# A planner with other latencies, loads that queue and an exclusion rule, and due times set by hand for 215 operations

## The chip, the cores and the metric

The kernel runs on one core of a Trainium2 chip. The metric is the device time of one execution in microseconds. Engines are named as the profile names them: PE is TensorE (PEld its weight loads), DVE is VectorE, ACT is ScalarE, POOL is GpSimd, SP is SyncE, which here issues nearly all DMAs (its queue is SPq in the rows).

## The reference, cut to what matters

A gated linear attention over 768 steps (4 batches, 8 heads, head size 48) feeds a two-layer network on 3072 tokens (384 to 2048 to 384), all in float32.

```python
for t in range(S):                       # S = 768
    cur = einsum('bhd,bhe->bhde', u * k_t, v_t)
    y[:, :, t] = einsum('bhd,bhde->bhe', r_t, state + cur)
    state = w_t[..., None] * state + einsum('bhd,bhe->bhde', k_t, v_t)
x = y.transpose(0, 2, 1, 3).reshape(3072, 384)
h = x @ w_in
g = maximum(h, 0) + alpha * minimum(h, 0)
out = g @ w_out
```

## The kernel before, in words

**Attention.** The 768 steps are cut in 12 blocks of 64, and two of the four batches are taken together, which gives 24 chunks q of 128 tokens. `load` (lines 385 to 398) fetches each chunk's decays (`wd`), keys and receptances in two layouts (`kr`, `rk`) and values (`nv`). `prep` runs two scans on DVE (lines 410 and 416), three or so products (406, 419, 422) and, from chunk 5 on, two products on POOL (440); ACT writes the diagonal blocks (`at`, 448). `scores`, `transposes` and `outputs` are bursts of small matmuls on PE (lines 467 and 513). For the first three chunks `spreads` (576) rearranges a part of the result on PE from a copy that ACT makes into `os` (579); the result goes to `x_0` (the tile `xw`, 589). POOL scales the running state (458).

**Network.** The hidden width is cut in 16 tiles j of 128. The weights come as 64-bit words, 768 KB a tile, into one of two buffers `raw` (line 634). ACT scales the low words in place (645), DVE makes the full weights `wf` from them in three passes (647, 650, 654). Later ACT copies the high part `wh` (665) and DVE makes the rest `wl` (666). Tokens are worked in 8 groups g of three chunks. Group 0 multiplies in plain float32 with `wf` (the units are listed in `FIRST`); groups 1 to 7 use three products of rounded parts, `wh`, `wl` and the two parts of x. A unit (g, j) is a product into the hidden tile (`moe_up`, PE line 684, three chunks wide), `pos` by ACT and DVE (689, 691), in groups 1 to 7 also `gh` and `gl` (695, 696), and two units later the product into the output (`moe_down`, line 709). `moe_out` copies and stores the result. `check_load` fetches decays and weights a second time, late in the program, for checks on ACT.

**What sets the order.** No engine's order is written out by hand. Each piece of work is declared by `op(engine, duration, function, reads, writes, ...)` of class `Plan` (line 107), which numbers it in the order of declaration, finds what it depends on from the keys it reads and writes, and gives it a due time where one is passed. The calls pass durations: 1.17 for a scan, 0.4 for an issue on SP, and `lat`, 2.2 for a weight tile. `order` (line 138) first hands due times back from each operation to those that it needs, then plays the program: at each moment each free engine starts, of the operations whose inputs are done, the one due first whose buffers are free. A load ends at `max(dma, end + DMA_LAT) + lat`, where `dma` is the end of the load before. Operations marked `lock` (DVE and POOL work that reads two tiles of SBUF) exclude one another on DVE and POOL. `order_late` (line 222) does this twice: after the first time each load is held back until `LEAD`, 10 us, before the planned start of the first operation that needs it. The resulting order of each engine is then emitted as it is: an engine runs its instructions strictly in that order, and waits at each for its inputs.

While the plan has PE idle before the first output product of chunk 2, filler matmuls on a constant tile are emitted (line 834, `FILL` and `FILL_MIN`), as many as the planned gap holds; at the start PE also runs 12 such matmuls (line 738).

Of the kernel before, what the change touches and what calls it, by code (L numbers as in the profile page):

```python
# [58 lines left out]
MODES = {("M", "Q"): 0.1, ("Q", "M"): 0.1}  # L59
DMA_LAT = 2.0  # L60
# [34 lines left out]
class Op:  # L95
    __slots__ = ("eng", "dur", "lat", "fn", "deps", "succ", "due", "lock", "takes", "uses", "kind", "n", "left",
                 "ready", "start", "after", "keys")


class Plan:  # L100
# [6 lines left out]
    def op(self, eng, dur, fn, r=(), w=(), lat=0.1, due=None, lock=False, kind=None, after=0.0):  # L107

        o = Op()
        o.eng, o.dur, o.lat, o.fn, o.due, o.lock, o.kind = eng, dur, lat, fn, due, lock, kind  # L110
        o.after = after
        o.n, o.deps, o.succ, o.takes, o.uses, o.start = len(self.ops), {}, [], [], [], None
        self.ops.append(o)
        o.keys = {*r, *w}
        keys = [(k if isinstance(k, tuple) else (k, None), k in w) for k in list(dict.fromkeys([*r, *w]))]
        for key, written in keys:
            t = key[0]
            if isinstance(t, Tensor) and t not in o.uses:
                o.uses.append(t)
                t.users += 1  # L120
                if t.first is None:
                    t.first = o.n
                    o.takes.append(t)
                else:
                    o.deps[t.first] = True
            if key in self.writer:
                o.deps[self.writer[key]] = True
            if written:
                for x in self.readers.get(key, ()):
                    o.deps.setdefault(x, False)  # L130
# [5 lines left out]
        o.deps.pop(o.n, None)  # L136
        return o

    def order(self):
        ops = self.ops  # L140
        for t in {t for o in ops for t in o.uses}:
            t.users = sum(t in o.uses for o in ops)
            t.ring.free, t.ring.given = list(range(len(t.ring.tiles))), 0
        for o in ops:
            o.succ = []
        for o in ops:
            for d in o.deps:
                ops[d].succ.append(o.n)
        for o in reversed(ops):
            late = [ops[s].due for s in o.succ if ops[s].deps[o.n]]  # L150
            late = min(late) - o.dur - o.lat if late else None
            o.due = late if o.due is None else o.due if late is None else min(late, o.due)
            if o.due is None:
                o.due = 1e6
        engines = ("PE", "DVE", "ACT", "POOL", "SP")
        free = dict.fromkeys(engines, 0.0)
        waiting = {e: [] for e in engines}
        ready = {e: [] for e in engines}
        ends, lock, dma, mode, now, todo = [], 0.0, 0.0, "M", 0.0, len(ops)
        for o in ops:  # L160
            o.left, o.ready = len(o.deps), o.after
            if not o.left:
                heapq.heappush(waiting[o.eng], (o.ready, o.n))
        while todo:
            while ends and ends[0][0] <= now:
                _, n = heapq.heappop(ends)
                for t in ops[n].uses:
                    t.users -= 1
                    if not t.users:
                        t.ring.free.append(t.slot)  # L170
            for e in engines:
                while waiting[e] and waiting[e][0][0] <= now:
                    _, n = heapq.heappop(waiting[e])
                    heapq.heappush(ready[e], (ops[n].due, n))
                if free[e] > now:
                    continue
                held, pick = [], None
                while ready[e]:
                    it = heapq.heappop(ready[e])
                    o = ops[it[1]]  # L180
                    if o.lock and (lock > now or e == "DVE" and any(
                            ops[n].lock and d < o.due for d, n in ready["POOL"] if free["POOL"] <= now)):
                        held.append(it)
                        continue
                    need = {}
                    for t in o.takes:
                        need.setdefault(t.ring, []).append(t)
                    if all(len(ts) <= len(g.free) and (not g.ordered or ts[0].ticket == g.given)
                           for g, ts in need.items()):
                        pick = o  # L190
                        break
                    held.append(it)
                for it in held:
                    heapq.heappush(ready[e], it)
                if pick is None:
                    continue
                o = pick
                for t in o.takes:
                    t.slot = t.ring.free.pop(0)
                    t.ring.given += 1  # L200
                o.start, dur, todo = now, o.dur, todo - 1
                if e == "PE":
                    dur += MODES.get((mode, o.kind[0]), 0.0)
                    mode = o.kind[1]
                end = now + dur
                free[e] = end
# [7 lines left out]
                heapq.heappush(ends, (end, o.n))  # L214
                for s in o.succ:
                    x = ops[s]
                    x.left -= 1
                    x.ready = max(x.ready, end)
                    if not x.left:
                        heapq.heappush(waiting[x.eng], (x.ready, s))  # L220
            if todo:
                assert any(t > now for t in free.values()) or ends or any(waiting.values()), "the rings are too short"
                times = [t for t in free.values() if t > now] + [w[0][0] for w in waiting.values() if w and w[0][0] > now]
                times += [ends[0][0]] if ends else []
                now = min(t for t in times if t > now)
        return sorted(ops, key=lambda o: (o.start, o.n))
# [11 lines left out]
def fast_path(tc, alpha_n, flag, dmaj, nat, u, ud, wts, alpha, out):  # L238
# [11 lines left out]
    with tc.tile_pool(name="const", bufs=1) as const, tc.tile_pool(name="psum", bufs=1, space=PSUM) as psum, \  # L250
# [13 lines left out]

        def w_low(j):
            if j not in wl:
                wl[j] = wpool.tile([P, 2, DM], F32R, name=f"wl{j}", tag=f"w{j - 1 if j else NF}")
# [29 lines left out]
        minus = const.tile([P, P], F32R, name="minus")  # L297
        r_pos = ring("pos", [P, GT], 3)
# [61 lines left out]

        def step(n):
# [3 lines left out]
            return (STEP if g > 0 else WHOLE) * (s1 - s0) / GS  # L365
# [34 lines left out]
        def prep(q):  # L400
# [27 lines left out]
            if q < U_BY_PE:  # L428
# [6 lines left out]
                op("PE", 0.9, sums, r=[rk, "u_dm"], w=[cp], kind="MM", due=due_att[q] - 3.5)  # L435
# [619 lines left out]
```

## Time and profile before

| what | value |
|---|---|
| runs | 508.67, 508.45, 504.23 us; median 508.45 us |
| profiled execution, first to last instruction | 507.8 us |
| median less this span | 0.65 us |
| instructions | 13048 |
| busy share of PE / DVE / ACT / POOL | 98% / 66% / 57% / 15% |
| moved by DMA | 72.40 MB, mean 143 GB/s |

The profile has no time of its own for the profiled execution beside the span. A busy share is an average over stages: PE can be busy at a lower granted clock or with fillers, and an engine that is 66% busy over the whole can have no free time in one stage. The views by stretch of time say which stage is which.

### The profile page before, as it was taken

Reading aid. Unit: us, or ns where it says so; the run is one execution under the profiler, and the core shown is the slowest. Engines: PE = TensorE matmul, PEld = TensorE weight load, DVE = VectorE, ACT = ScalarE, POOL = GpSimd, SP = SyncE. Lnnn points to the kernel's source line nnn. Section 1 sums busy time; section 2 is a strip of 40 time slices with the busy share of each in tenths; the row PEclk is TensorE's granted clock in tenths of the full one; section 3 lists DMA queues with packets and bytes.
Section 4 is the critical chain, followed back from the end, with each engine's and each line's share of the span. In section 5 each row is a group of like instructions: output and inputs, shape, how many; then the busy total and the mean of one; then the engine's idle time right before and its main releaser. Section 6 shows DMA issues by size and latency. Waiting matters only on the chain.

```text
span 507.8 us, 13048 instructions
## 1 busy us (share of the span) xinstructions
PE 496.1 (98%) x5406; PEld 458.7 (90%) x5406; DVE 337.6 (66%) x602; ACT 291.5 (57%) x746; POOL 74.0 (15%) x103
## 2 busy tenths in 40 slices
PE   8999998999999999999999999999999999999995
PEld 8876664689999999999999999999999999999995
DVE  6899997999987564956478474855556353443332
ACT  4866574563363535456585765776677676553331
POOL 2010333233014010222014020030000000000000
PEclk9999998999999999999999999999999999999999
DMA  8648884561163311736157461756445441210001
GB/s 300 234 179 294 298 297 166 181 185 43 43 178 86 104 52 65 185 99 224 60 171 215 126 207 46 258 168 205 146 140 196 139 159 63 71 44 21 1 3 52
DMA packets 27107, 72.40 MB, mean 143 GB/s; under 512 B 3680, under 2 KB 8224, under 8 KB 27040
## 3 DMA queue, kind: packets, MB, share of 16 engines
q1 hardware_dynamic: 26656, 71.19, 43.5%
q8 instruction: 44, 0.72, 0.6%
q10 hardware_dynamic: 384, 0.30, 0.2%
q14 instruction: 23, 0.19, 0.1%
HBM read 64.70 MB, written 4.72 MB: 137 GB/s over the span
## 4 chain that ended last, share of the span: by engine, by line
PE 70%; DVE 11%; DMA 9%; ACT 5%; issue 3%; SPq 2%; ACTq 0%; DVEq 0%
PE bank L684 31%; PE op L709 30%; DMA raw<-in_wts_dram 6%; PE bank L467 6%; DMA kr<-in_dmaj_dram 2%; ACT at L448 1%; DVE cx L650 1%; DVE wf L654 1%; DVE suf L410 1%; DVE pos L691 1%; DVE kr L419 1%; PE bank L513 1%; DVE gl L696 1%; DVE kr L422 1%; SPq L621 1%
## 5 line engine op out<-in xcount | busy, mean ns | idle before, releaser
L684 PE MATMUL bank<-x,wh 128*128 128x384 f32 x672 | 191.3, 338 | 0.0
L689 ACT ACTIVATE pos<-bank,alpha_n 128x384 f32<-128x384 f32 (+1 forms) x133 | 75.4, 569 | 104.5 <-PE bank L684 102.3
L691 DVE SCALAR_TENSOR_TENSOR pos<-bank,pos 128x384 f32<-128x384 f32 (+1 forms) x133 | 71.6, 538 | 89.4 <-ACT pos L689 89.2
L684 PEld LDWEIGHTS bank<-x,wh 128*128 128x128 f32 x672 | 123.0, 188 | 1.2
L709 PE MATMUL op<-wh,gl 128*128 128x384 f32 x336 | 113.0, 336 | 1.0 <-DVE gl L696 0.7
L709 PE MATMUL op<-wh,gh 128*128 128x384 f32 x336 | 113.1, 337 | 0.0
L709 PE MATMUL op<-wl,gh 128*128 128x384 f32 x336 | 112.5, 335 | 0.0
L684 PE MATMUL bank<-x,wl 128*128 128x384 f32 x336 | 112.4, 335 | 0.0
L696 DVE TENSOR_TENSOR gl<-pos,gh 128x384 fp32r<-128x384 f32 x112 | 67.1, 599 | 54.8 <-ACT gh L695 54.8
L695 ACT CAST gh<-pos 128x384 fp32r<-128x384 f32 x112 | 57.5, 514 | 53.5 <-DVE pos L691 52.7
L709 PEld LDWEIGHTS op<-wh,gl 128*128 128x128 f32 x336 | 63.1, 188 | 2.9 <-DVE gl L696 2.9
L709 PEld LDWEIGHTS op<-wh,gh 128*128 128x128 f32 x336 | 63.1, 188 | 0.1
L684 PEld LDWEIGHTS bank<-x,wl 128*128 128x128 f32 x336 | 63.1, 188 | 0.0
L709 PEld LDWEIGHTS op<-wl,gh 128*128 128x128 f32 x336 | 63.1, 188 | 0.0
L458 POOL TENSOR_TENSOR St<-St,pc_all 128x192 f32<-128x192 f32 x44 | 23.8, 562 | 248.7 <-DVE St L611 209.8
L448 ACT ACTIVATE at<-twin,cd 128x64 f32<-128x64 f32 x192 | 52.6, 343 | 0.9 <-PE bank L467 0.7
L684 PE MATMUL bank<-xw,wf 128*128 128x384 f32 (+2 forms) x126 | 35.9, 425 | 2.3 <-DVE wf L654 2.3
L709 PE MATMUL op<-wf,pos 128*128 128x384 f32 x96 | 35.4, 499 | 0.0
L410 DVE TENSOR_TENSOR_SCAN suf<-wd,low 128x528 f32<-128x528 f32 x24 | 30.9, 1287 | 3.9 <-DMA wd<-in_dmaj_dram 3.9
L416 DVE TENSOR_TENSOR_SCAN wd<-wd,low 128x528 f32<-128x528 f32 x24 | 33.4, 1391 | 0.1
L684 PEld LDWEIGHTS bank<-xw,wf 128*128 128x128 f32 x126 | 20.9, 193 | 13.1 <-DVE wf L654 3.1
L440 POOL TENSOR_TENSOR rk<-rk,u_bc 128x384 f32<-128x384 f32 x19 | 20.3, 1069 | 84.1 <-DMA rk<-in_nat_dram 49.3
(81 smaller groups left out, 530.0 us busy)
## 6 DMA issues: line engine op xcount, KB each, us to landing
raw<-in_wts_dram SPq DMA_DIRECT2D x32, 768.0 KB, 5.1
kr<-in_dmaj_dram SPq DMA_DIRECT2D x24, 512.0 KB, 3.9
rk<-in_nat_dram SPq DMA_DIRECT2D x19, 384.0 KB, 3.7
wd<-in_dmaj_dram SPq DMA_DIRECT2D x24, 264.0 KB, 2.8
raw<-in_dmaj_dram SPq DMA_DIRECT2D x12, 528.0 KB, 4.2
nv<-in_nat_dram SPq DMA_DIRECT2D x24, 256.0 KB, 4.9
out_dram<-os SPq DMA_DIRECT2D x44, 96.0 KB, 2.2
x<-x SPq DMA_DIRECT2D x28, 72.0 KB, 4.6
```

Source lines behind the costliest of these rows:

```text
L410: op("DVE", 1.17, lambda: nc.vector.tensor_tensor_scan(out=suf.ap[:, ::-1], data0=w.ap[:, ::-1], data1=low[:, ::-1], initial=0.0, op0=ALU. ...
L416: op("DVE", 1.17, lambda: nc.vector.tensor_tensor_scan(out=w.ap, data0=w.ap, data1=low, initial=0.0, op0=ALU.mult, op1=ALU.max), r=["low"] ...
L440: op("POOL", 1.0, lambda i=i: nc.gpsimd.tensor_tensor(out=rk.ap[:, 0:HD], in0=rk.ap[:, 0:HD], in1=u_bc if i == 0 else rk.ap[:, HD:], op=AL ...
L448: nc.scalar.activation(out=at.ap[:, o, p, :], in_=twin, func=AF.Copy, scale=cd.ap[:, o * NP + p:o * NP + p + 1])
L458: op("POOL", 0.6, lambda i=i: nc.gpsimd.tensor_tensor(out=St[b][:, i, :, 0:D], in0=St[b][:, i, :, 0:D], in1=pc_all[:, q, i::2].unsqueeze(2 ...
L467: nc.tensor.matmul(yb[q][i].ap[rows, cols], start=(i, rows.start) not in opened[q], stop=stop, skip_group_check=True, **kw)
L684: nc.tensor.matmul(hp.ap[:, ts], lhsT=a, rhs=b[:, k, ts], start=(i == 0), stop=(i == m - 1))
L689: op("ACT", 0.15 + 0.33 * share, lambda: nc.scalar.activation(out=pos.ap[:, ts], in_=hp.ap[:, ts], func=AF.Relu, scale=alpha_n[:, j:j + 1] ...
L691: op("DVE", 0.07 + 0.4 * share, lambda: nc.vector.scalar_tensor_tensor(out=pos.ap[:, ts], in0=hp.ap[:, ts], scalar=0.0, in1=pos.ap[:, ts], ...
L695: op("ACT", 0.43, lambda: nc.scalar.copy(out=gh.ap, in_=pos.ap), r=[pos], w=[gh])
L696: op("DVE", 0.47, lambda: nc.vector.tensor_tensor(out=gl.ap, in0=pos.ap, in1=gh.ap.bitcast(F32), op=ALU.subtract), r=[pos, gh], w=[gl], lo ...
L709: nc.tensor.matmul(ops_[s], lhsT=a.ap[:, ts], rhs=w, start=(j == 0 and i == 0), stop=(j == NF - 1 and i == len(todo) - 1))
```

## The change

A few of the planner's costs change (going from 64-wide to 128-wide matmuls, `spreads`, `transposes` and the first 12 matmuls); what follows an operation on another engine now waits for a lag by engine (`TAIL`), or for one given with the operation (`part`). A load's end is counted from its start, which for an issue of 0.4 us is the same as before. `order` is rewritten around a list of events, and POOL now comes before DVE: a POOL operation with `lock` is issued at once and starts when DVE's running one ends, and DVE starts no `lock` operation until 0.1 us before POOL's ends. `dues` adds a number of `TUNE` to the due time of 215 operations, counted in order of declaration, and hands it back to what they need. `LEADS` changes the 10 us of lead for six loads: 744 is the load of weight tile 0, 23 and 29 are values of chunks 1 and 3, 33 and 34 decays and keys of chunk 5, 35 is u. `THREE` is 16 (`NF`) and `APART` is empty, and with these values the new branches that use them compute what stood there before.

```diff
-MODES = {("M", "Q"): 0.1, ("Q", "M"): 0.1}
-DMA_LAT = 2.0
+MODES = {("M", "Q"): 0.1, ("Q", "M"): 0.08}
+DMA_LAT = 2.4
+TAIL = {"PE": 0.2, "DVE": 0.118, "ACT": 0.133, "POOL": 0.083, "SP": 0.033}
+TUNE = {
+    5: 5.64, 10: 5.26, 123: -7.58, 134: -6.64, 138: -11.21, 144: -0.6, 145: -9.26, 146: -1.09, 149: 16.13, 152: -13.79, 154:
...
+    2.32, 887: -12.08, 888: 2.78, 889: 2.15, 892: 15.07, 893: 1.44, 898: -5.37, 899: 2.18, 901: 10.36, 903: 4.39, 905: -1.46, 906:
...
+LEADS = {
+    23: -1.51, 29: -5.91, 33: 8.76, 34: -0.82, 35: 5.78, 744: -4.77,
+}
+APART = ()
+THREE = NF
...
+        def wait(n, data, key):
+            x = self.ops[n]
+            if n != o.n and not (x.eng == eng and eng != "SP"):
+                o.lag[n] = max(o.lag.get(n, -9.0), x.part.get(key[0], TAIL[x.eng]) if data else TAIL[x.eng])
...
+    def dues(self, tune):
...
+            late = min(late) - o.dur - o.lat if late else 1e6
+            o.due = min(late, 1e6 if o.own is None else o.own) + tune.get(o.n, 0.0)
...
-        engines = ("PE", "DVE", "ACT", "POOL", "SP")
+        engines = ("PE", "POOL", "DVE", "ACT", "SP")
...
-                if o.lock:
-                    lock = end
-                if e == "SP":
-                    dma = max(dma, end + DMA_LAT) + o.lat
-                    end = dma
-                else:
-                    end += o.lat + (0.15 if e == "PE" else 0.06)
...
+                    o.start, dur, todo = now, o.dur, todo - 1
+                    if o.lock and e == "POOL" and lock["DVE"] > now:
+                        o.start = lock["DVE"]
...
+                    if o.lock:
+                        lock[e] = end - (0.1 if e == "POOL" else 0.0)
+                        push(events, (lock[e], 2, "POOL" if e == "DVE" else "DVE"))
+                    if e == "SP":
+                        dma = max(dma, now + DMA_LAT) + o.lat
+                        end = dma
...
     def order_late(self, lead, until):
 
+        self.dues(TUNE)
         self.order()
...
-                o.after = max(o.after, need - lead)
+                o.after = max(o.after, need - lead - LEADS.get(o.n, 0.0))
...
-            op("PE", 0.45, products, r=[(kr, 0), "ident"], w=[kp, "kn"], kind="MM", due=due_att[q] - 3.0)
+            op("PE", 0.36, products, r=[(kr, 0), "ident"], w=[kp, "kn"], kind="MM", due=due_att[q] - 3.0, tag=("t", q))
...
-                op("PE", 0.75, spreads, r=[sp, (tmp, s % 2, 0), (tmp, s % 2, 1)], w=yb[q], kind="MM")
+                op("PE", 1.29, spreads, r=[sp, (tmp, s % 2, 0), (tmp, s % 2, 1)], w=yb[q], kind="MM", part={yb[q][0]: -0.45})
...
+        def place_low(j):
+            return NF if j == THREE % NF else (j - 1) % NF
...
+        def parted(g, j):
+            return g > 0 or j >= THREE
...
-        op("PE", 4.4, wm, r=[(tmp, "warm")], w=[wm_t], kind="MM", due=0.0)
+        op("PE", 4.5, wm, r=[(tmp, "warm")], w=[wm_t], kind="MM", due=0.0)
```

In this numbering 900 and 901 are the ACT and the DVE part of `pos` of unit (0, 11), 805, 807 and 808 the ACT pass (645), the second and the last DVE pass (650, 654) of weight tile 12, and 810 the ACT pass of tile 13.

## Rows read from the trace of the kernel before

**Rows 1.** The page, its first part: busy time, share, instructions.
```profile
span 507.8 us, 13048 instructions
...
PE 496.1 (98%) x5406; PEld 458.7 (90%) x5406; DVE 337.6 (66%) x602; ACT 291.5 (57%) x746; POOL 74.0 (15%) x103
```

**Rows 2.** Busy by stretch: from:to, length, engines' busy us (instructions), granted clock, DMA share, GB/s.
```profile
3.90:18.79 14.89, 13.50 (x270) 12.20 (x269) 14.81 (x24) 9.95 (x38) 0.44 (x6) 1.00 0.82 306
18.79:79.80 61.01, 60.78 (x672) 42.09 (x666) 56.53 (x94) 38.91 (x96) 14.20 (x16) 1.00 0.74 262
79.80:82.15 2.35, 0.04 (x1) 0.00 (x0) 1.48 (x3) 2.35 (x9) 0.00 (x0) 1.00 0.28 110
82.15:85.40 3.25, 3.25 (x7) 1.91 (x8) 3.25 (x4) 1.12 (x3) 2.57 (x2) 0.66 0.68 225
85.40:88.00 2.60, 2.60 (x8) 1.41 (x8) 2.60 (x4) 0.58 (x1) 0.00 (x0) 0.77 0.40 125
...
116.00:496.90 380.90, 379.85 (x4061) 371.60 (x4059) 229.38 (x426) 218.84 (x556) 44.91 (x55) 1.00 0.38 117
```

**Rows 3.** The chain that ended last, 70 to 86 us: start, length, what.
```profile
71.33 7.86 DMA raw<-in_wts_dram
...
79.27 0.91 ACT raw L645
80.18 0.47 ACT pos L689
...
81.15 0.96 DVE wf L654
```

**Rows 4.** Instructions of PE, 82 to 93 us: start, length, line, tiles, count.
```profile
82.15 3.23 PE L684 MATMUL bank<-xw,wf 128*128 128x384 f32 x6 [2.31 <-DVE wf L654]
...
87.82 0.55 PE L513 MATMUL bank<-ident,kr 112*128 112x112 f32 x4
88.20 2.11 PE L684 MATMUL bank<-xw,wf 128*128 128x384 f32 x6
90.15 2.10 PE L709 MATMUL op<-wf,pos 128*128 128x384 f32 x6
92.18 0.46 PE L467 MATMUL bank<-kr,St 64*64 64x64 f32 x16
```

**Rows 5.** Instructions of ACT and DVE in order of time, 72 to 78 us.
```profile
72.20 0.95 ACT L645 ACTIVATE raw<-raw 128x768 int32<-128x768 uint32 x1
...
73.91 1.69 DVE L650 SCALAR_TENSOR_TENSOR cx<-raw,cx 128x768 int32<-128x768 int32 x1
```

**Rows 6.** The chain that ended last, 3 to 18 us.
```profile
3.28 8.59 DMA raw<-in_wts_dram
...
11.90 0.95 ACT raw L645
...
15.74 0.19 ACT os L579 x2
```

**Rows 7.** Instructions of PE, 12 to 19 us.
```profile
12.54 0.69 PE L467 MATMUL bank<-at,nv 64*64 64x64 f32 x32
...
14.27 0.62 PE L834 MATMUL op<-os 128*128 128x128 f32 x4
15.96 1.52 PE L576 MATMUL bank<-os,os 128*128 128x64 f32 x12 [1.07 <-ACT os L579]
17.32 0.44 PE L834 MATMUL op<-os 128*128 128x128 f32 x2
...
18.79 0.94 PE L684 MATMUL bank<-xw,wf 128*128 128x128 f32 x6
```

**Rows 8.** DMA issues, 0 to 110 us: tiles, count, KB each, median us to landing.
```profile
raw<-in_wts_dram SPq DMA_DIRECT2D x16, 768.0 KB, 4.6
```

**Rows 9.** Instructions of DVE, 14 to 55 us: the last pass of tile 0, one blocked scan.
```profile
14.86 0.95 DVE L654 CUSTOM_DVE_ANT_0 wf<-raw,cx 128x1536 uint16<-128x1536 uint16 x1
...
54.22 2.04 DVE L410 TENSOR_TENSOR_SCAN suf<-wd,low 128x528 f32<-128x528 f32 x1
```

More of the change, by code (lines that the diff above doesn't have):

```diff
@@ L95 @@
 class Op:
[L96 to L97 removed]
+    __slots__ = ("eng", "dur", "lat", "fn", "deps", "lag", "succ", "due", "own", "lock", "takes", "uses", "kind", "n", "left",
+                 "ready", "start", "after", "keys", "tag", "part", "rings", "_a0")
 class Plan:
@@ L140, in order @@
+    def order(self, until=1e9):
         ops = self.ops
-        for t in {t for o in ops for t in o.uses}:
-            t.users = sum(t in o.uses for o in ops)
-            t.ring.free, t.ring.given = list(range(len(t.ring.tiles))), 0
+        rings = {}
         for o in ops:
-            o.succ = []
+            for t in o.takes:
+                t.users = 0
+                t.ring.free, t.ring.given = list(range(len(t.ring.tiles))), 0
         for o in ops:
-            for d in o.deps:
-                ops[d].succ.append(o.n)
@@ L156, in order @@
+            o.rings = list(need.items())
+            o.left, o.ready, o.start = len(o.deps), o.after, None
+        engines = ("PE", "POOL", "DVE", "ACT", "SP")
         free = dict.fromkeys(engines, 0.0)
-        waiting = {e: [] for e in engines}
         ready = {e: [] for e in engines}
-        ends, lock, dma, mode, now, todo = [], 0.0, 0.0, "M", 0.0, len(ops)
+        held = {e: [] for e in engines}
+        lock = {"DVE": 0.0, "POOL": 0.0}
+        dma, mode, todo, count = 0.0, "M", len(ops), 0
@@ L160, in order @@
+        events = []
         for o in ops:
-            o.left, o.ready = len(o.deps), o.after
             if not o.left:
-                heapq.heappush(waiting[o.eng], (o.ready, o.n))
+                events.append((o.ready, 0, o.n))
+        heapq.heapify(events)
+        push, pop = heapq.heappush, heapq.heappop
         while todo:
[L165 to L170, printed above, removed]
@@ L221, in order @@
[L221 to L226, printed above, removed]
+            now = events[0][0]
+            if now > until:
+                break
@@ new lines, in order @@
+            dirty = set()
+            while events and events[0][0] <= now + 1e-9:
+                _, what, n = pop(events)
+                if what == 0:
+                    e = ops[n].eng
+                    push(ready[e], (ops[n].due, n))
+                    dirty.add(e)
+                elif what == 1:
+                    for t in ops[n].uses:
+                        t.users -= 1
+                        if not t.users:
+                            t.ring.free.append(t.slot)
+                            dirty.update(engines)
+                else:
+                    dirty.add(n)
@@ L228, in order_late @@
+            if todo and not events:
+                assert False, "the rings are too short"
+        return sorted((o for o in ops if o.start is not None), key=lambda o: (o.start, o.n))
     def order_late(self, lead, until):
+        self.dues(TUNE)
         self.order()
@@ L702, in moe_down @@
             g, s0, s1, j = units[m]
+            three = parted(g, j)
             for s in range(s0, s1):
```

188 lines of the change are left out of this document (107 added, 81 removed), and 19 rows, old and new, of the table TUNE.

## The prediction

> **What bounds the kernel now.** I read the busy times of the whole span first, then the same by stretch, then the chain that ended last through the stretches where PE was not full, and at those places the engines in order of time. Over the whole, PE is busy for 496.1 of 507.8 us and, its own weight loads aside, no other engine for more than 337.6 [rows 1]. So the time is PE's work, plus what PE loses; a plan can win only the losses. By stretch there are three kinds of them [rows 2]. From 3.90 to 18.79 DVE is full (14.81 of 14.89) and prepares the first chunks and weight tiles; PE waits for it, with small work and fillers between. From 18.79 to 79.80 PE is full (60.78 of 61.01), and DVE nearly so (56.53). From 79.80 to 82.15 PE stands still, and then runs until 88.00 at a granted clock of 0.66 and 0.77. From 116.00 to 496.90 PE misses 380.90 - 379.85 = 1.05 us in all, too little to plan for.
>
> The stall at 79.80 is the place to understand. PE waits 2.31 us for the weights of tile 12 [rows 4]. Their inputs had long been there: ACT's pass over that tile began at 72.20, and DVE's middle pass ran from 73.91 to 75.60 [rows 5]. But DVE had `pos` of unit 11 ahead of the last pass, that `pos` needed ACT's part, and ACT had ahead of it the pass over tile 13, whose load was issued at 71.33 and took 7.86 us [rows 3], where the median of 16 such loads is 4.6 [rows 8]. So ACT sat until 79.27, did the tile (0.91), then `pos` (0.47), and DVE's last pass came at 81.15 [rows 3]. One late load stood first in line on one engine, and by way of the order stopped two more.
>
> **The change part by part.** No instruction is added or removed but fillers, and none becomes shorter; costs, lags and `TUNE` only alter the order, and `LEADS` the moment of six loads. So I price the losses that another order can take away, on the profiled execution, and move the result to the median, which is 0.65 above its span.
>
> *The stall and its slow matmuls.* The wait is 2.35 us, from 79.80 to 82.15 [rows 2]. After it, six matmuls into the hidden tile and six into the output take 87.82 - 82.15 = 5.67 us, where the next such pair takes 92.18 - 88.20 = 3.98 [rows 4]: 1.69 more, at granted clocks that are 0.66 and 0.77 on average, a mix of the 2.4 and 1.2 GHz levels, after a stretch in which PE did nothing. Together 4.0. `TUNE` puts DVE's `pos` of unit 11 (operation 901) 10.36 later and leaves the last pass over tile 12 (808) as it was, so the pass should now go ahead of `pos`: from 75.60 on it needs only its turn, and PE wanted the tile at 79.80. I take the whole 4.0. The ends are 0, if some other late load does the same elsewhere, and 4.0. What hides the rest: DVE has 61.01 - 56.53 = 4.48 us free in the 61 us before [rows 2].
>
> *The start.* ACT's copy of chunk 0 into `os` ran at 15.74 [rows 6], though the matmuls that make it began at 12.54 and took 0.69 [rows 7]. Between lie ACT's wait for the first weight tile, which ended at 11.90 after a landing of 8.59 us [rows 6], and work of chunk 1 that this wait pushed back. PE meanwhile ran fillers, 0.62 and 0.44, and stood idle 1.07 [rows 7]: 2.1 us between 14.27 and 17.69 with nothing of use. The first hidden product came at 18.79 [rows 7], and its weights were there at 14.86 + 0.95 = 15.81 [rows 9], so at most 18.79 - 15.81 = 3.0 can go. The new cost of `spreads`, the lags and the numbers of `TUNE` among the first 160 operations bear on just these steps. Bounds 0 and 3.0; the nearest row is PE's useless 2.1, and I take 2.0, as DVE has no free time here to give more.
>
> *The load of weight tile 0* is held back by `LEADS` (744: a lead of 5.23 instead of 10). In this trace its first user started at 11.90, which would put the issue at 6.67, 3.39 later than 3.28 [rows 6]; in the plan, where it lands sooner, the user is earlier and the shift smaller. The gain of an undisturbed load for chunk 1 is in the 2.0. I take 0 for the rest; ends: 0 and 3.4 lost, if the later load lands as much later. Past it on SP's queue move the loads of chunk 1 only.
>
> *Exclusion.* A scan on DVE at 54.22 took 2.04 us [rows 9] where the plan has 1.17; such meetings are what the new rule is about. It lets POOL go first, at most one POOL product of planned 1.0 us ahead of a DVE operation. On the path this is nothing while PE is full; the cover is DVE's 4.48 us free, and if the new order loses more than that on DVE, PE is late by what is over. Gain and loss I bound by 1 us each way, and take 0.
>
> *Fewer fillers* save nothing by themselves, being gaps already. *After 116 us* the new lags reorder a little; bounds 1.05 gained and 1.05 lost, taken 0.
>
> Sum: 508.45 - 4.0 - 2.0 = 502.4.
>
> One rule stands against the first term. All 16 weight loads had a median of 4.6 us to landing [rows 8], as the plan's 2.4 + 2.2 has it for an empty queue, but this one took 7.86, with others issued right behind it. The Trainium skill, page "DMA: Bandwidth & Descriptors", section "Queues, rings and completion order", says that completion is not in order of issue on one queue, and "Issuing engines are not separate DMA queues" that transfers interleave on the same 16 engines. The plan ends one load after the other. [...]
>
> **The rivals.** *The late load comes back.* A weight load again lands 3 us after its plan and stands before something that PE needs; the stall moves, and its 4.0 stay: 508.45 - 2.0 = 506.4. For it: the model of a load's end is unchanged but for `LEADS`, and in both places where PE lost time ACT stood before a weight load [rows 3, 6]. Against it: this stall needed three things in a row, and `TUNE` undoes one.
>
> *Held-back first weights make it slower.* Place: ACT and DVE before 16 us. If tile 0 is issued at 6.67 and still takes 8.59 us, it lands at 15.3; the three passes after it end near 15.3 + 0.95 + 0.95 = 17.2 without queueing, against 15.81, and with ACT blocked the first product is up to 3.4 late: 508.45 + 3.4 = 511.9 with the stall kept. It decides from a landing after 14.9, when the 3.0 of slack between 15.81 and 18.79 is eaten. Against it: in the stretch 306 GB/s were moved [rows 2], and a load issued later meets fewer others.
>
> *Nothing to measure.* PE is full from 18.79 because tiles come just in time. A start that is 2 us earlier is lost again if DVE, with 93% of its time used there, cannot follow; and what the stall gave is lost to small waits. Then 508, less 0 to 1.
>
> *More than forecast.* All 3.0 of the start, the 4.0, and the 1 of exclusion: 508.45 - 8.0 = 500.4.
>
> **How the numbers follow.** Forecast 0.50, with its own range 500.5 to 505; more than forecast 0.10; the late load 0.20; nothing 0.10; slower 0.10. The range leaves out about a tenth on each side: 499.0 to 508.8. A measurement of this kernel can tell about 1% from no change, which is 503.4 and 513.5. Faster than that: three quarters of the forecast and the whole of the better case, 0.38 + 0.10 = 0.48. Same: the rest of the forecast, the late load and most of the case of nothing, 0.40. Slower: 0.12, the slower rival with 0.02 for an unforeseen wait in the tuned order; the runs of before themselves spread by 4.4 us.
>
> **What would show it.** The stall gone: no PE wait over 1 us between 70 and 120 us, a granted clock of 1.00 through, the last pass over tile 12 (654) ahead of `pos` of unit 11 (691) on DVE. The start: the first hidden product near 16.8 instead of 18.79, fewer fillers. The first steady unit of group 1 then lies 6 us earlier, and the rest of the span is a copy of the old one. I am wrong if PE again waits for `wf` or ACT for `raw` in group 0, if the first product is later than 18.79, or if losses appear after 116 us, where I expect none.

## The result, and the profile after

The changed kernel takes 510.87 us (median of 18 runs, 507.67 to 513.71), the one before 507.10 us (18 runs beside it, 504.23 to 512.70): a ratio of 1.0073 [1.0055, 1.0092]. Every ratio in this document leaves out the few runs that lie over 1.5% above the fastest of their kernel. By it after is slower by 3.7 us, where 502.4 us was forecast, and the time lies above the range of 499.0 to 508.8.

The profiled execution of after took 510.79 us, 1.7 more than its span. The same 1.7 around before's span of 507.8 makes 509.5 of that execution, 2.4 above before's median. So the two profiles lie closer together than the two kernels do; what is lost is read from the experiments more than from this pair.

The page of after, first part, answers [rows 1]:

```profile
span 509.1 us, 13051 instructions
...
PE 496.7 (98%) x5406; PEld 459.9 (90%) x5406; DVE 342.6 (67%) x602; ACT 291.8 (57%) x746; POOL 79.4 (16%) x103
```

As many instructions on each engine as before, and DVE busy for 5.0 us more with the same 602. Busy times of after by stretch, with the columns of [rows 2]:

```profile
3.90:19.83 15.93, 14.94 (x214) 14.30 (x214) 13.71 (x21) 9.37 (x39) 0.48 (x6) 0.89 0.72 265
19.83:80.00 60.17, 59.27 (x590) 40.06 (x589) 57.81 (x91) 36.72 (x78) 8.81 (x10) 1.00 0.73 251
80.00:100.00 20.00, 18.92 (x311) 12.52 (x310) 19.32 (x35) 14.60 (x42) 7.70 (x8) 1.00 0.62 204
...
120.00:160.00 40.00, 39.64 (x576) 38.11 (x576) 39.73 (x68) 19.67 (x56) 9.50 (x10) 1.00 0.38 115
```

The first hidden product comes at 19.83, not 18.79. From there to 80 us DVE has 60.17 - 57.81 = 2.36 us free, where [rows 2] left 4.48; between 120 and 160 us it has 0.27 of 40, where before had 2.37. What PE waited for in the whole span (us in total, times, longest):

```profile
PE bank L815 <- POOL os L382: 1.7, 1, 1.7
PE bank L759 <- issue: 1.2, 1, 1.2
PE bank L503 <- DVE rk L476: 1.0, 1, 1.0
PE bank L759 <- DVE wf L727: 0.9, 2, 0.7
```

The wait of 2.31 us for a weight tile [rows 4] is gone, and with it the low clock behind it: 1.00 in every stretch after 19.83. In its place stand several waits of about 1 us (the first row is the start of the kernel).

The low clock has not gone from the profile, though. The first row by stretch has 0.89, where [rows 2] had 1.00: PE stood idle for 0.99 up to 8.67, and from 11 to 13 us it was granted 0.50, the lower of its two levels (1.2 of 2.4 GHz). Eight filler matmuls took 2.07 there:

```profile
8.67 1.05 PE L503 MATMUL bank<-u_dm,rk 128*128 128x2 f32 x8 [0.99 <-DVE rk L476]
11.16 2.07 PE L920 MATMUL op<-os 128*128 128x128 f32 x8
```

A part of the later first product may thus belong to this one execution. In another profile with the same start (`after_two_scans_twice` below, which differs only from 40 us on) PE idled 1.15 at the same place, yet the clock stayed at 1.00, the eight fillers took 1.16, and the first hidden product came at 18.40; its keys of chunk 0 had also come 0.6 sooner. Before's own four profiles with an unchanged start have it between 17.54 and 18.79. Why the clock fell in one and not in the other stays open.

The late load itself is still there, and costs PE 0.66:

```profile
79.35 0.93 ACT L718 ACTIVATE raw<-raw 128x768 int32<-128x768 uint32 x1 [1.62 <-DMA raw<-in_wts_dram]
...
82.90 2.17 PE L759 MATMUL bank<-xw,wf 128*128 128x384 f32 x6 [0.66 <-DVE wf L727]
```

One more thing is to be seen on DVE alone. Instructions of DVE in after (start, length, line):

```profile
5.16 0.20 DVE L483 RECIPROCAL low<-suf 128x8 f32<-128x8 f32 x1
5.40 1.26 DVE L486 TENSOR_TENSOR_SCAN wd<-wd,low 128x528 f32<-128x528 f32 x1
...
9.86 1.25 DVE L480 TENSOR_TENSOR_SCAN suf<-wd,low 128x528 f32<-128x528 f32 x1
11.14 0.20 DVE L483 RECIPROCAL low<-suf 128x8 f32<-128x8 f32 x1
11.27 0.65 DVE L476 TENSOR_TENSOR rk<-kr 128x512 f32<-128x512 f32 x1
11.83 1.25 DVE L486 TENSOR_TENSOR_SCAN wd<-wd,low 128x528 f32<-128x528 f32 x1
13.00 0.67 DVE L489 TENSOR_TENSOR kr<-kr,suf 128x512 f32<-128x512 f32 x1
...
26.64 0.56 DVE L720 TENSOR_SCALAR cx<-raw 128x768 int32<-128x768 int32 x1
27.11 0.45 DVE L568 COPY_PREDICATED at<-mask,bank 128x256 f32<-128x256 int32 x1
27.44 0.96 DVE L723 SCALAR_TENSOR_TENSOR cx<-raw,cx 128x768 int32<-128x768 int32 x1
28.54 0.96 DVE L727 CUSTOM_DVE_ANT_0 wf<-raw,cx 128x1536 uint16<-128x1536 uint16 x1
...
36.27 0.55 DVE L720 TENSOR_SCALAR cx<-raw 128x768 int32<-128x768 int32 x1
36.86 0.96 DVE L723 SCALAR_TENSOR_TENSOR cx<-raw,cx 128x768 int32<-128x768 int32 x1
```

Read starts, not lengths. From 720 to an operation that does not need it is 0.47 (26.64 to 27.11), from 720 to 723, which reads its result, 0.59 (36.27 to 36.86). From 723 to 727, which needs it, is 1.10; to another operation put in between it is 0.86 (shown below, where the lag is put back). A scan to the reciprocal that needs it is 1.28 (9.86 to 11.14), a scan to a product that does not 1.17 (11.83 to 13.00); behind the reciprocal it is 0.24 (5.16 to 5.40) and 0.13 (11.14 to 11.27). So an operation right behind the one whose result it needs, a dependent pair below, starts 0.12 us later than another would, and 0.22 later behind 723. Counted over the DVE instructions of the whole trace, such pairs stand side by side 4 times in before and 42 times in after: 10 of 720 and 723, 12 of 723 and 727, 10 of 480 and 483, 10 of 483 and 486. By these prices that is 30 x 0.12 + 12 x 0.22 = 6.2 us of DVE, against 0.5 before. In the diff it is the first line of `wait`: no lag is noted where `x.eng == eng`. Before, every dependence had one, on the same engine too.

### The profile page after: what moved, and what is told of

It reads as the page before. It is cut to its first block, busy times and chain, and to the rows that moved or that the text cites. A ratio compares the mean times of both kernels' runs of the same rounds, so it can differ in the third digit from the quotient of the medians.

```text
span 509.1 us, 13051 instructions
## 1 busy us (share of the span) xinstructions
PE 496.7 (98%) x5406; PEld 459.9 (90%) x5406; DVE 342.6 (67%) x602; ACT 291.8 (57%) x746; POOL 79.4 (16%) x103
## 4 chain that ended last, share of the span: by engine, by line
PE 79%; DVE 13%; DMA 4%; ACT 2%; issue 2%; SPq 1%; DVEq 0%
PE op L785 35%; PE bank L759 34%; PE bank L537 7%; DVE cx L723 2%; DVE wf L727 2%; PE bank L583 1%; DVE cx L720 1%; DMA x<-x 1%; DVE pos L766 1%; DMA kr<-in_dmaj_dram 1%; DVE suf L480 1%; ACT at L518 1%; DMA raw<-in_wts_dram 1%; DVE wd L486 1%; DVE kr L489 1%
## 5 line engine op out<-in xcount | busy, mean ns | idle before, releaser
L759 PE MATMUL bank<-x,wh 128*128 128x384 f32 x672 | 189.4, 336 | 1.8 <-issue 1.2
L785 PE MATMUL op<-wh,gh 128*128 128x384 f32 x336 | 115.0, 342 | 0.0
L528 POOL TENSOR_TENSOR St<-St,pc_all 128x192 f32<-128x192 f32 x44 | 25.7, 600 | 239.7 <-DVE St L682 173.0
L518 ACT ACTIVATE at<-twin,cd 128x64 f32<-128x64 f32 x192 | 49.9, 344 | 2.2 <-DVE cd L513 2.0
L510 POOL TENSOR_TENSOR rk<-rk,u_bc 128x384 f32<-128x384 f32 x19 | 22.8, 1199 | 89.5 <-DMA rk<-in_nat_dram 73.8
L480 DVE TENSOR_TENSOR_SCAN suf<-wd,low 128x528 f32<-128x528 f32 x24 | 34.0, 1417 | 3.9 <-DMA wd<-in_dmaj_dram 3.9
L486 DVE TENSOR_TENSOR_SCAN wd<-wd,low 128x528 f32<-128x528 f32 x24 | 31.8, 1323 | 0.3
```

The lines of the kernel that those rows point to most:

```text
L480: op("DVE", 1.17, lambda: nc.vector.tensor_tensor_scan(out=suf.ap[:, ::-1], data0=w.ap[:, ::-1], data1=low[:, ::-1], initial=0.0, op0=ALU. ...
L486: op("DVE", 1.17, lambda: nc.vector.tensor_tensor_scan(out=w.ap, data0=w.ap, data1=low, initial=0.0, op0=ALU.mult, op1=ALU.max), r=["low"] ...
L510: op("POOL", 1.0, lambda i=i: nc.gpsimd.tensor_tensor(out=rk.ap[:, 0:HD], in0=rk.ap[:, 0:HD], in1=u_bc if i == 0 else rk.ap[:, HD:], op=AL ...
L518: nc.scalar.activation(out=at.ap[:, o, p, :], in_=twin, func=AF.Copy, scale=cd.ap[:, o * NP + p:o * NP + p + 1])
L528: op("POOL", 0.6, lambda i=i: nc.gpsimd.tensor_tensor(out=St[b][:, i, :, 0:D], in0=St[b][:, i, :, 0:D], in1=pc_all[:, q, i::2].unsqueeze(2 ...
L759: nc.tensor.matmul(hp.ap[:, ts], lhsT=a, rhs=b[:, k, ts], start=(i == 0), stop=(i == m - 1))
```

## The experiments

A letter in an expectation names a theory of that expectation. "Planner alone" is after with `TUNE` and `LEADS` left out; the reference kernel of every ratio is before.

### Is the stall what it was said to be

Before, run again with a profile, and before with one change in the finished order: ACT's pass over tile 13 behind `pos` of unit 11.

```diff
+        plan.ops[810].start = plan.ops[900].start + 0.4
+        order.sort(key=lambda o: (o.start, o.n))
```

before_again: 

> The kernel before, unchanged, for a second profile. Theory A (the stall before the weights of tile 12 is an accident of the profiled execution, and the typical run lacks most of it): no PE wait over 1 us between 70 and 90 us, span near 505. Theory B (the stall belongs to the order): a PE wait of 2 us or more near 80 us again, span near 507.8.

before_pos_first: 

> The kernel before, with one ACT operation moved: the pass over weight tile 13 goes behind pos of unit 11 instead of ahead of it. Theory A (the stall near 80 us is made by that order: ACT waits for a late load in front of work that DVE and PE need): no PE wait over 0.5 us between 76 and 84 us, and 1 to 4 us faster than the kernel before, ratio 0.992 to 0.998. Theory B (the stall is an accident of some executions, or is made by the load itself): ratio 0.999 to 1.001.

The first took 512.17 us in its one execution, and PE again waited for weights there: 1.15 for tile 12 by the same chain, and 1.38 for the next weight tile. The granted clock stayed at 1.00 through both, so neither the 2.35 nor the 1.69 of the prediction came again. The second gave 0.998 [0.995, 1.001], 1.0 us; in its profile, of a span of 501.5, the stretch is clean:

```profile
80.00:100.00 20.00, 20.00 (x197) 13.51 (x196) 19.28 (x31) 10.98 (x24) 8.54 (x6) 1.00 0.60 201
```

So the chain of [rows 3] is real and is undone by one exchange on ACT, but over repeated runs it is worth about 1 us, not 4.0, and the interval also holds no change.

### The first loads

First exchanges among the first nine issues of SP: after with before's order, and before with after's.

```diff
+        for i, n in enumerate((18, 19, 21, 22, 20, 744, 749, 15, 25)):
+            plan.ops[n].start = 0.3 * i
+        order.sort(key=lambda o: (o.start, o.n))
```

after_first_loads_as_before: 

> The kernel after, with only the first nine DMA issues of SP put back into the order of the kernel before (decays 0, keys 0, decays 1, keys 1, values 0, weight tiles 0 and 1, alpha, keys 2); the order of all engines else is kept. Theory A (the loss is made by the order of the first loads: keys of chunk 0 land 2 to 3 us later because decays 1, keys 1 and keys 2 share the transfer with them): first hidden product near 18.5 instead of 19.83, time 1.5 to 3 us below the kernel after, so a ratio to the kernel before of 1.001 to 1.004. Theory B (the tuned due times or POOL going first make many small waits after 20 us): the time stays within 0.7 us of the kernel after, ratio 1.006 to 1.009.

before_first_loads_as_after: 

> The kernel before, with only the first nine DMA issues of SP in the order of the kernel after (decays 0, decays 1, keys 0, keys 1, alpha, keys 2, values 0, weight tiles 0 and 1). Theory A (order of the first loads): 1.5 to 3 us slower than the kernel before, ratio 1.003 to 1.006. Theory B (the loss is made later): ratio 0.999 to 1.002.

Measured 1.0163 [1.0117, 1.0210] and 1.0083 [1.0049, 1.0117]: each order is worse in the other kernel. The first mixes in another effect: `alpha_n` landed at 12.32 instead of 9.33, and ACT waited 6.97 us for it. The second says that after's order of loads costs before about 4 us. That price is not after's own: before has the product that waits for the keys ahead of the second scan, so that DVE idled 1.41 us there, and its granted clock was 0.63 from 10 to 14 us. Where after pays, its trace shows (SP's issues, then DVE):

```profile
0.93 0.89 SPq L460 DMA_DIRECT2D wd<-in_dmaj_dram  x2
1.86 0.91 SPq L461 DMA_DIRECT2D kr<-in_dmaj_dram  x2
...
7.92 0.69 DVE L476 TENSOR_TENSOR rk<-kr 128x512 f32<-128x512 f32 x1 [1.26 <-DMA kr<-in_dmaj_dram]
```

The keys of chunk 0 stand behind the decays of chunk 1. DVE, with nothing else to do, waits 1.26 us for them; in before it used them at 5.31 without a wait. Next, after with these two exchanged, and then with chunk 17's `scores` (operation 598) due 3 us later as well:

```diff
+        plan.ops[19].start, plan.ops[21].start = plan.ops[21].start, plan.ops[19].start
+        order.sort(key=lambda o: (o.start, o.n))
```

after_keys0_first: 

> The kernel after, with two loads exchanged on SP's queue: keys of chunk 0 go ahead of decays of chunk 1, and all else keeps its order. Theory A (loads land in order of issue, keys 0 come about 1 us late in the kernel after, DVE stands idle for them and never gets that time back, as DVE is what bounds the first 110 us): DVE's idle time in the first 20 us falls by about 1 us, and the time by 1 to 1.5 us, ratio to the kernel before 1.004 to 1.006. Theory B (a late start is made good behind, the loss comes from small waits after 60 us that have other causes): within 0.5 us of the kernel after, ratio 1.006 to 1.009.

after_keys0_q17_later: 

> The kernel after with keys of chunk 0 loaded ahead of decays of chunk 1, as before, and with the burst of small matmuls of chunk 17 (operation 598) due 3 us later, so that it no longer follows that of chunk 16 within 4 us. Theory A (two bursts so close use up PE's instructions faster than they are fetched, which shows as PE idle for no wait, 0.5 to 1.8 us near 324 us in each profile of the kernel after and its variants, and in none of the kernel before): that idle time is gone, and the time is 0.5 to 1.5 us below the run with keys 0 first alone, ratio to the kernel before 1.001 to 1.004. Theory B (the idle time is an accident of the profile): still there, ratio 1.004 to 1.006.

Measured 1.0046 [1.0015, 1.0077] and 1.0031 [1.0010, 1.0053]. Both edits together take 2.1 us away by the ratios, from 1.0073 to 1.0031, and the interval is clear of after's; how much is the first one's, these intervals don't settle. The pairs are 42 in both, as in after. In the profile of the first, DVE is idle for 4.46 us of the first 20 instead of 6.09.

### Is DVE the bound

Two scans (480, or 410; operations 212 and 237) are emitted twice, with the same result: 2.5 us more of DVE, near 40 and 54 us in before, near 46 and 60 in after.

```diff
+                if o.n in (212, 237):
+                    o.fn()
```

after_two_scans_twice: 

> The kernel after, with the first DVE scan of chunks 4 and 5 (1.25 us each, planned near 42 and 55 us) issued twice, which gives the same values and takes 2.5 us more of DVE. Theory A (in the kernel after DVE bounds the stretch from 20 to 110 us): 2 to 2.5 us slower than the kernel after, ratio to the kernel before 1.011 to 1.013. Theory B (PE or the loads bound it): under 1 us slower, ratio 1.006 to 1.009.

before_two_scans_twice: 

> The kernel before, with the same two scans issued twice. Theory A (in the kernel before PE bounds this stretch, DVE has some 4 us free): 0 to 1 us slower than the kernel before, ratio 1.000 to 1.002. Theory B (DVE bounds the kernel before as well): 2 to 2.5 us slower, ratio 1.004 to 1.005.

After went from 1.0073 to 1.0097 [1.0061, 1.0133], 1.2 us; before to 1.0036 [1.0003, 1.0069], 1.8 us. In before some of the 2.5 us is paid at the end, so DVE's free time does not cover all of it. In after the interval also holds no change. The price per us of DVE is thus 0.7 in before, roughly, with an interval of 0.06 to 1.4.

### Which part of the planner

Four kernels: the planner alone; after without `LEADS` but with `TUNE`; the planner alone with before's exclusion rule; the planner alone with before's lags, on the same engine too (0.25 behind PE, 0.16 behind DVE, ACT and POOL).

```diff
-        self.dues(TUNE)
+        self.dues({})
...
-            if n != o.n and not (x.eng == eng and eng != "SP"):
-                o.lag[n] = max(o.lag.get(n, -9.0), x.part.get(key[0], TAIL[x.eng]) if data else TAIL[x.eng])
+            if n != o.n:
+                o.lag[n] = TAIL[x.eng]
```

planner_alone: 

> The kernel after without the added due times and the changed leads (both tables empty); the new planner with its lags, costs and exclusion rule orders everything. Theory A (the tables, which bring the first loads in another order, make the loss): ratio to the kernel before 0.998 to 1.002. Theory B (the new planner's rules, POOL first above all, make it): ratio 1.006 or more, and DVE busy for as long as in the kernel after, about 5 us more than before.

after_no_leads: 

> The kernel after with the changed due times and without the six changed leads. Theory A (the leads change only the order on SP's queue, since the chip issues a load as soon as its turn and its buffer come, and the two tables were made for one another): slower than the kernel after, ratio 1.010 or more. Theory B (holding the first weight tile back is part of the loss): faster than the kernel after, ratio 1.004 or less.

planner_alone_old_lock: 

> The new planner without the two tables, and with the exclusion rule of the kernel before (one lock for both engines, DVE gives way only to POOL work that is due earlier). Theory A (POOL going first is what makes the new planner's order worse): ratio to the kernel before 1.003 or less, against 1.010 for the new planner alone. Theory B (the lags make it): 1.006 to 1.012.

planner_alone_old_lags: 

> The new planner without the two tables, and with the waits after an operation of the kernel before (0.25 us after PE, 0.16 after the other engines, on the same engine too) in place of the lags by engine. Theory A (POOL first makes it worse): 1.006 to 1.012. Theory B (the lags, shorter than before, plan work closer together than the chip allows): 1.003 or less.

| lags | exclusion rule | ratio |
|---|---|---|
| before's | before's | 1 (before) |
| before's | new | 0.9943 [0.9921, 0.9964] |
| new | before's | 1.0215 [1.0183, 1.0246] |
| new | new (planner alone) | 1.0101 [1.0073, 1.0129] |
| new, with `TUNE` and `LEADS` | new (after) | 1.0073 [1.0055, 1.0092] |
| new, with `TUNE` only | new | 1.0293 [1.0255, 1.0332] |

The first row is before itself, whose planner also has the old costs; between the second, third and fourth one part changes at a time. The lags lose 1.6% (1.0101 against 0.9943) and the exclusion rule wins 1.1% (1.0215 against 1.0101). Measured against the first row, where the costs change as well, it is 2.1 and 0.6%; what the costs alone do was not run. The two tables bring 0.3%, with intervals that overlap. The tables belong together: without the six leads, the 215 due times are worth less than nothing. And one kernel beats before and after: the new planner with the old lags and no table at all, 503.73 us.

### Which part of the lags

The same-engine lag alone is put back into the planner alone (0.16 us); before's lags across engines without a same-engine lag; and then the same-engine lag on DVE only, with either set of lags across engines. The diff is of the first; for DVE only its condition is `eng == "DVE"`.

```diff
+            if n != o.n and x.eng == eng and eng != "SP":
+                o.lag[n] = 0.16
-            if n != o.n and not (x.eng == eng and eng != "SP"):
+            elif n != o.n:
```

planner_alone_same_engine_lag: 

> The new planner without its two tables, with one lag put back: 0.16 us between an operation and one that needs it on the same engine; the lags across engines stay the new ones. Theory A (the loss is DVE's: pairs of dependent passes that now stand next to each other, 0.12 or 0.22 us each): in the finished order such pairs fall from 47 to about 10, so some 5 us less of DVE time at 0.5 to 0.7 us of time per us of DVE: ratio to before 0.993 to 0.999, against 1.010 for the planner alone. Theory B (the loss is from the shorter lags between engines, so that other engines wait): 1.006 or more.

planner_alone_old_lags_not_same: 

> The new planner without its two tables, with before's lags across engines and no lag on the same engine: the other half. In the finished order 51 dependent pairs stand next to each other on DVE. Theory A: ratio 1.006 to 1.015. Theory B: 0.998 or less, near the 0.994 of the run with all the old lags.

planner_alone_dve_lag: 

> The planner alone with its new lags across engines, and the same-engine lag of 0.16 us for DVE only (none on PE, ACT, POOL). Theory A (dependent passes side by side on DVE): as with the lag on every engine, 0.998 to 1.005. Theory C (it is the lag on PE or ACT that matters, or any other order would do): 1.007 to 1.013, as the planner alone.

planner_alone_old_lags_dve: 

> The planner alone with before's lags across engines, and its same-engine lag for DVE only. Theory A: most of the way from 1.018 (no lag on the same engine) to 0.994 (lag on every engine): 0.993 to 1.001. Theory C: 1.010 or more.

| lags across engines | on the same engine | pairs side by side | their us of DVE | ratio |
|---|---|---|---|---|
| new | none (planner alone) | 47 | 6.7 | 1.0101 [1.0073, 1.0129] |
| new | all engines | 10 | 1.3 | 1.0014 [0.9992, 1.0035] |
| new | DVE only | 11 | 1.4 | 1.0036 [1.0004, 1.0067] |
| before's | none | 51 | 7.2 | 1.0180 [1.0156, 1.0204] |
| before's | all engines | 10 | 1.2 | 0.9943 [0.9921, 0.9964] |
| before's | DVE only | 10 | 1.2 | 0.9990 [0.9960, 1.0020] |

This is the clearest answer of the study, and it holds for the planner without its tables. The same-engine lag decides, with either set of lags across engines, and DVE's alone brings 0.65 of 0.87% and 1.9 of 2.4%. The lags across engines matter less, and their sign depends on it: the new ones are 0.8% better than before's without a same-engine lag, and 0.7% worse with it. How the lag works in the order of DVE is seen with it put back on all engines (lines are 2 higher than in after):

```profile
26.84 0.95 DVE L725 SCALAR_TENSOR_TENSOR cx<-raw,cx 128x768 int32<-128x768 int32 x1
27.70 0.48 DVE L768 SCALAR_TENSOR_TENSOR pos<-bank,pos 128x128 f32<-128x128 f32 x2
28.10 0.20 DVE L485 RECIPROCAL low<-suf 128x8 f32<-128x8 f32 x1
28.21 0.91 DVE L729 CUSTOM_DVE_ANT_0 wf<-raw,cx 128x1536 uint16<-128x1536 uint16 x1
...
30.21 0.53 DVE L722 TENSOR_SCALAR cx<-raw 128x768 int32<-128x768 int32 x1
30.66 0.68 DVE L478 TENSOR_TENSOR rk<-kr 128x512 f32<-128x512 f32 x1
31.26 0.95 DVE L725 SCALAR_TENSOR_TENSOR cx<-raw,cx 128x768 int32<-128x768 int32 x1
```

Here the planner has put something between 725 and 729, and between 722 and 725: 0.86 to the next start instead of 1.10, and 0.45 instead of 0.59. What PE waits for without the lag is DVE's late `pos`: 2.9 us in one wait in the planner alone, 0.5 with the lag put back. In the kernel with before's lags across engines and none on the same engine:

```profile
PE bank L759 <- DVE pos L766: 3.8, 3, 3.1
PE op L785 <- DVE pos L766: 1.4, 1, 1.4
```

against 1.0 and 0.5 in the longest such waits of the kernel with all the old lags.

The lag also changes what DVE does first. These are the planner alone (DVE, then PE's first hidden product), and behind the dots the same with the lag put back on all engines:

```profile
5.20 0.21 DVE L483 RECIPROCAL low<-suf 128x8 f32<-128x8 f32 x1
5.44 1.26 DVE L486 TENSOR_TENSOR_SCAN wd<-wd,low 128x528 f32<-128x528 f32 x1
6.61 0.67 DVE L476 TENSOR_TENSOR rk<-kr 128x512 f32<-128x512 f32 x1
19.35 0.94 PE L759 MATMUL bank<-xw,wf 128*128 128x128 f32 x6
...
5.17 0.21 DVE L485 RECIPROCAL low<-suf 128x8 f32<-128x8 f32 x1
5.39 0.69 DVE L478 TENSOR_TENSOR rk<-kr 128x512 f32<-128x512 f32 x1
6.00 1.25 DVE L488 TENSOR_TENSOR_SCAN wd<-wd,low 128x528 f32<-128x528 f32 x1
16.57 1.43 PE L761 MATMUL bank<-xw,wf 128*128 128x128 f32 x6
```

Without the lag the scan goes right behind the reciprocal that it needs, and the product that PE's first sums need (476, in the second kernel 478) comes 1.2 us later. Of the 3.8 us between these two profiled spans (510.0 and 506.2), 2.8 are there at the first hidden product. The other kernels without tables agree: with the lag on DVE it comes between 16.39 and 17.96, without it between 19.29 and 20.30. These are single profiles, and before's own start varies by 1.25, so this says where much of the loss appears, not its exact size.

### The same in the changed kernel itself: two misses

After with the same-engine lag of 0.16; and after with its order kept but on DVE, where in a dependent pair side by side the second operation changes places with the one behind it, if that one needs neither.

after_same_engine_lag: 

> The changed kernel with its tables, and the same lag of 0.16 us on the same engine put back. The pairs fall from 42 to 13. Theory A: below the changed kernel, ratio 0.999 to 1.004, unless the tables, which were made for the other lags, now place something badly. Theory B: 1.006 or more.

after_pairs_apart: 

> The changed kernel with its order kept on every engine but DVE; there, where a pass stands right behind the one that it needs and the pass behind both needs neither, the second and the third are exchanged, on the finished order. Pairs fall from 42 to 27 or fewer, by the rows' 0.12 and 0.22 us each some 3.5 us less of DVE. Theory A: 1.5 to 3 us faster than the changed kernel, ratio to before 1.001 to 1.005. Theory B: no change, 1.006 to 1.009.

Measured 1.0129 [1.0089, 1.0168] and 1.0134 [1.0109, 1.0158]. Neither is faster than after, though the pairs fell from 42 to 13 and to 19; the second is clearly slower, and the interval of the first just touches after's. The trace of the second shows what such an exchange costs at one place (in after 727 ran here at 25.44, ahead of 568):

```profile
23.34 0.96 DVE L723 SCALAR_TENSOR_TENSOR cx<-raw,cx 128x768 int32<-128x768 int32 x1
25.95 0.45 DVE L568 COPY_PREDICATED at<-mask,bank 128x256 f32<-128x256 int32 x1 [1.66 <-PE bank L537]
26.30 0.95 DVE L727 CUSTOM_DVE_ANT_0 wf<-raw,cx 128x1536 uint16<-128x1536 uint16 x1
```

To save 0.22 the last pass over a tile got behind an operation that waits 1.66 for PE. PE's idle time under "issue" also rose, from 1.2 to 4.0 us. So this run does not tell whether a pair by itself costs the end anything. What it does say is that a finished order can't be mended pair by pair: the lag has to be known when the order is made. In the first of the two it was, but under due times found for a plan without it: the same planner with the lag and without the tables has 1.0014, so with the lag in, the tables lose over 1%.

## Why the prediction was wrong

*The step that failed* is the sentence that lags "only alter the order", with the covers behind it. It is true of each instruction's length and false of the time from one start to the next on DVE. The change part listed the new lag by engine and passed over that the old one held on the same engine too. Priced at 0, leaving it out cost 0.87% in the planner without its tables, 1.0101 against 1.0014: 4.4 us, more than the 3.7 that after lost. That it is after's own loss is argued, not shown. In after with its tables the lag put back won nothing, and what did win there, 2.1 us, was an exchange of two loads and a later burst, with all 42 pairs left in place.

How the lag reaches the end is only partly shown. The pairs' own price in the same two kernels is 6.7 - 1.3 = 5.4 us of DVE, enough at 0.8 us of time per us. But with before's lags across engines 2.4%, 12 us, hang on 6.0 us of pairs, and taking pairs apart afterwards won nothing. Of the 3.8 us between the two profiles, 2.8 are there at the first hidden product, behind another first order on DVE. A plan that counts such steps too short takes DVE to be further on than it is, and orders all engines by that; this fits all of these, but is only argued.

*The cover.* While PE is full, DVE's 4.48 us free were taken to hide small losses on DVE. Two doubled scans in that stretch cost before 1.8 us of 2.5, with an interval of 0.2 to 3.5. A sum of free time over 61 us does not say that it lies where a loss needs it.

*The stall, 4.0 predicted.* The mechanism was right in every link: the wait and the low clock are gone, the last pass goes ahead, and one exchange in before does the same. The size was wrong: 1.0 us over repeated runs, and at most 2.5 by the interval. A second profile of before had 1.15 in that wait and no low clock, so the 4.0 was one execution's. That execution also lay above before's median, at 509.5 by after's 1.7 around the span; the 0.65 that I set between span and time came from a median of other runs.

*The start, 2.0 predicted.* Nothing of it came: the first hidden product is 1.04 later in the profile, a part of which may be the low clock there, and at 18.40 in the profile with a clock of 1.00, where 16.8 was forecast. I looked at ACT and the weight tile, held that on SP's queue "the loads of chunk 1 only" move past it, and took DVE as having "no free time here". It was given some: in after the decays of chunk 1 go ahead of the keys of chunk 0, which are issued third, and DVE waits 1.26 us for them. The weight load itself did as the rival with the first weights said, but not its price: it was issued at 4.74 and landed at 13.05, ahead of the 14.9 from which that rival decides. Its 511.9 is near the measured time for another reason.

*Exclusion, 0 with bounds of 1 us each way.* Measured 1.1% in the planner without its tables, 5.8 us gained (1.0215 to 1.0101), outside its bounds. One long scan [rows 9] was taken as the measure of a rule that changes every meeting of two engines.

*`LEADS`, 0 with an end of 3.4 lost.* Without the six leads after is 2.2% slower, so they could not be priced apart from `TUNE`.

*After 116 us, 0 with 1.05 either way.* Within its bounds: PE misses 0.36 from 116 to 160 us and 1.26 behind it, 1.62 where it missed 1.05. But 1.24 of that is one idle time near 324 us that before does not have (below).

*The signs of being wrong* came: PE waits 0.66 for `wf` and ACT 1.62 for `raw` in group 0, the first product is later than 18.79, and the idle time near 324 us is a loss after 116.

*The rule weighed* (the Trainium skill, page "DMA: Bandwidth & Descriptors", section "Queues, rings and completion order") allows loads to complete out of their order of issue. No trace here shows it: in after the first twelve loads of SP's queue landed in order, from 3.77 to 16.93, with the keys of chunk 0, third in line, at 7.90, and in none of the 20 traces does a transfer of that queue with a recorded landing land ahead of one issued before it. The late load did come back, as the first rival has it: issued at 73.52, it took 5.75 us. But it cost 0.66, not 4.0.

## What to carry to other kernels

A planner's lag between dependent operations of one engine is no detail: leave it out, and the order fills with dependent neighbours on the engine that is nearly full. The busy shares hardly show it (67% of the span for DVE without the lag, 66% with it); the distance from start to start does. Change a planner's costs first with all hand-set due times empty, compare, and fit the tables last; a table fitted to one set of costs can cost more than it won under another. And before a stall in one profiled execution is priced in full, set that execution beside the median of its runs with what lies around its span.

## What the runs showed of the hardware

*A dependent neighbour on DVE* starts 0.12 us later than an independent one behind the 128x768 pass of line 720 (0.59 against 0.47 from start to start), a 128x528 scan (1.29 against 1.17) or the 128x8 reciprocal (0.23 against 0.11), and 0.22 later behind the 128x768 pass of line 723, which reads two tiles (1.10 against 0.87). These are typical values; the traces with more than a few such pairs agree.

*PE stood idle under "issue"* for 1.24 us near 324 us in after, with all its inputs there, behind two dense bursts of small matmuls, of which the second began 4.1 us after the first (315.63 and 319.77; 5.8 in before: 313.35 and 319.13):

```profile
323.12 0.33 PE L759 MATMUL bank<-x,wl 128*128 128x384 f32 x1
324.69 0.33 PE L759 MATMUL bank<-x,wh 128*128 128x384 f32 x1 [1.24 <-issue]
```

The same gap, 0.5 to 1.8 us, is in the four other traces that keep PE's order of after there; with the second burst 5.7 us behind the first it was gone. Two transfers of queues named "instruction" lie between 320 and 325 us, while 344 GB/s were moved; before has one there and no gap. The Trainium skill, page "Runtime: NRT & Kernel Launch", section "Instruction fetch mechanics", says that an engine fetches its instructions in blocks over a DMA queue of its own while it runs, mostly hidden. That a late block is the cause here fits, but no run tested it.
